# Three rounded products in place of float32 for most attention scores, and a later conversion of three weight blocks, in a one-core attention and feed-forward kernel

## The chip, the cores and the metric

The kernel runs on one core of one Trainium2 chip. Its engines are TensorE (PE in the profile; PEld is its weight load), VectorE (DVE), ScalarE (ACT), GpSimd (POOL) and SyncE (SP), which here issues most of the DMA transfers. Each engine works through its own queue in order; semaphores tie the queues together. The metric is the time of one execution in microseconds (us), as the median of the runs; a profiled execution gives the trace.

## The reference

Causal attention over 2 batches, 12 heads, 448 positions and 64 columns a head, then two feed-forward layers over the 768 columns, the first with a low-rank mixing of the positions in front, the second behind a layer norm:

```python
scores = scale * np.matmul(q, k.transpose(0, 1, 3, 2))
scores = np.where(mask, -1000000000.0, scores)
scores = scores - np.max(scores, axis=-1, keepdims=True)
attn = np.exp(scores); attn = attn / (np.sum(attn, axis=-1, keepdims=True) + 1e-09)
x = np.matmul(attn, v)                                    # heads side by side: 768 columns
h = x.transpose(0, 2, 1) @ U @ V                          # U: 448 x 32, V: 32 x 448
u = x + h.transpose(0, 2, 1); x = u + np.maximum(u @ w1a, 0.0) @ w2a
xn = (x - mean(x)) / np.sqrt(var(x) + 1e-06) * g_ln;      x + np.maximum(xn @ w1b, 0.0) @ w2b
```

The inputs q and k are drawn with a standard deviation of about 0.5. The weights arrive as 64-bit floats (the kernel reads their bits and makes 32-bit words of them).

## The kernel before, in words

The attention stage is written out by hand; the two feed-forward layers behind it are ordered by a planner (class `Plan`), which the change does not touch. The first 108 us of the profile are the attention stage.

Two heads form a *pair*, 12 pairs in all. Positions are cut into four blocks of 112. The main loop is `for n in range(NPT)`, here called round 0 to round 11. In round n, PE transposes the exponentials of pair n (`a_transpose`, L441), turns the finished outputs of pair n-1 back to positions by rows (`a_tokens`, L483), multiplies q and k of pair n+2 (`a_scores`, L387), multiplies pair n's transposed weights with v (`a_values`, L471), and from round 3 on adds the mixing of the positions for pair n-3 (`a_mix2`, L571). In odd rounds `a_sum` (L535) makes the small matrix `ts` that this mixing uses; its last step is a subtraction on DVE (L542). DVE takes the row maxima of pair n+2 from PSUM (`a_max`, L405, eight instructions, with the `ts` subtraction after the fifth), then the reciprocals (L461), and copies part of the transposes to SBUF (`pt`, L445). ACT takes the exponentials of pair n+1 (L422), spread over the round: one ahead of each of its copies in `a_transpose`, three more, then what `ahead("high", n)` puts in, then the rest. The transposes of pair n+1 need all eight of them.

Scores are float32 products. The two heads of a pair lie in the two halves of the 128 rows, so that their products use different halves of PE. Each float32 product is recorded as two passes.

While attention runs, the first four weight blocks of the first layer are loaded and converted. A block takes four steps: a load of 768 KB (SP), the upper half of each word (`upper`, ACT, L258), joining it with the middle (`joined`, DVE, L266), and `split` into a rounded high part (ACT, L299) and the low part `w - high` (L296). The products of the feed-forward layers take a weight and an activation each as such a high and a low part in float32r, three products for one. `ahead` sets in which round these steps are issued: the site "high" lies behind the sixth exponential and in front of `a_max`, the site "values" at the start of `a_values`. Before the change, upper halves go out in rounds 1, 3, 5, 7, joining in 2, 4, 6, 8, splitting in 3, 5, 7, 9, and the low parts of these four blocks are made by POOL. Two raw tiles hold the loads, so a joining is followed by the load of a later block.

The first products with these weights start in round 11: `mm1(early[0], 0, ...)` with block 0, after the loop `early[1]` with block 1 and `early[2]` with block 2 (L603). Between them stand the last pair's tokens, its own mixing (`a_mix1`, L553) and the last `a_mix2`. PSUM has 8 banks, taken in turn; a bank can be written again when all that read it are done.

q and k of a pair come as one tile of 128 rows and 2 x 448 columns, in three buffers; `a_load(n + 3)` at the end of `a_scores(n)` refills the buffer just read.

Of the kernel before, what the change touches and what calls it, by code (L numbers as in the profile page):

```python
# [8 lines left out]
F32 = mybir.dt.float32  # L9
F32R = mybir.dt.float32r  # L10
# [12 lines left out]
R = 32  # L23
# [14 lines left out]
PLACE_U, PLACE_W = 96, 192  # L38
MASKED = -8.0e9
LATE = 4  # L40
SLOTS = (1, 5, 6, 2, 7, 3, 4)

OFF = [Q * i * (i + 1) // 2 for i in range(NQ + 1)]
# [153 lines left out]
def block_kernel(ctx: ExitStack, tc: tile.TileContext, qk, v, U, V4, w1a, w2a, w1b, w2b, g_ln, out):  # L197
# [25 lines left out]
    def bank(name, i=None):  # L223
        if i is None:
            turn[0] += 1
        return ps.tile([P, 512], F32, tag="bank", name=name)
# [24 lines left out]
    def load_part(t, src, queue, r0=0):  # L251
        rows, cols = src.shape
        queue.dma_start(out=t[r0:r0 + rows].bitcast(U16)[:, :4 * cols - 1], in_=src.bitcast(U16)[:, 1:])
# [72 lines left out]

    def ahead(site, n):

        if site == "values" and n in (2, 4, 6, 8):
            plan.emit(first_w1[n // 2 - 1][2])  # L330
            plan.emit(next(loads))
        if site == "high" and n in (1, 3, 5, 7, 9):
            j = (n - 3) // 2
            if j >= 0:
                plan.emit(first_parts[j][0])
                plan.emit(first_parts[j][1], nc.gpsimd)
            if n < 9:
                plan.emit(first_w1[j + 1][1])

    qk_p = attn.enter_context(tc.tile_pool(name="qk_p", bufs=2))  # L340
    s_p = attn.enter_context(tc.tile_pool(name="s_p", bufs=6))
# [1 line left out]
    x_p = attn.enter_context(tc.tile_pool(name="x_p", bufs=2))  # L343
    ot_p = attn.enter_context(tc.tile_pool(name="ot_p", bufs=5))
    row_p = attn.enter_context(tc.tile_pool(name="row_p", bufs=3))
    sel_p = attn.enter_context(tc.tile_pool(name="sel_p", bufs=1))

    sc_t, qk_t, v_t, s_t, den_t, pt_t, x_t, o_t, rd_t, nm_t = ({} for _ in range(10))
    pairs = [(b, p) for b in range(B) for p in range(NP)]
# [2 lines left out]
    def a_load(n):  # L352

        if n >= NPT:
            return
        r = qk_t[n] = qk_p.tile([P, 2, S], F32, tag="qk", name=f"qk{n}", bufs=3)
        src = qk[n].rearrange("p (a h s) -> p a h s", a=2, h=2)
        for part in (slice(0, 2 * Q), slice(2 * Q, S)) if n == 0 else (slice(0, S),):
            for h in range(2):
                rows = slice(h * D, (h + 1) * D)  # L360
                (nc.scalar if h and n == 0 else nc.sync).dma_start(out=r[rows, :, part], in_=src[rows, :, h, part])

    def a_load_v(n):
        if n >= NPT:
            return
        t = v_t[n] = qk_p.tile([Q, NQ, 2, D], F32, tag="v", name=f"v{n}", bufs=3)
        nc.sync.dma_start(out=t, in_=v[n].rearrange("p (j h d) -> p j h d", j=NQ, h=2))
# [6 lines left out]
    def a_scores(n):  # L374
        if n >= NPT:
            return
        t = qk_t.pop(n)
        sc_t[n] = [bank("sc") for _ in JOBS]
        at = {(h, i): (acc, o) for acc, job in zip(sc_t[n], JOBS if n else FIRST) for h, i, o in job}
        if n:  # L380
            turn_of = lambda h, i: (3, 2, 0, 1).index(i)
        else:
            turn_of = lambda h, i: (i, 0) if i > 1 else (-1 - h, -i)
        for (h, i), (acc, o) in sorted(at.items(), key=lambda t: turn_of(*t[0])):
            w = (i + 1) * Q
            r = slice(h * D, (h + 1) * D)
            nc.tensor.matmul(  # L387
                acc[:Q, o:o + w], t[r, 0, i * Q:(i + 1) * Q], t[r, 1, :w], start=True, stop=True,
            )
        a_load(n + 3)  # L390


    def turns_of(n):
# [20 lines left out]
    def a_exp(n):  # L414

        if n >= NPT:
            return
        den = den_t[n] = small.tile([Q, 2, NQ], F32, tag="den", name=f"den{n}")
        nm, sb = nm_t.pop(n), s_t[n]
        for _, h, i, _ in turns_of(n):  # L420
            s = sb[h][:, OFF[i]:OFF[i + 1]]
            nc.scalar.activation(  # L422
                s, s, AF.Exp, bias=nm[:, h, i:i + 1], scale=-1.0, accum_out=den[:, h, i:i + 1]
            )
            yield
# [52 lines left out]
    def a_tokens(n):  # L478

        ot, rd = o_t[n], rd_t.pop(n)  # L480
        acc = bank("xt")
        for i in range(NQ):
            nc.tensor.transpose(acc[:Q, i * P:(i + 1) * P], ot[:, i * Q:(i + 1) * Q], ident)  # L483
        b, p = pairs[n]
        if p % 2 == 0:
            x_t[b, p // 2] = x_p.tile([Q, NQ, 2 * P], F32, tag="x", name=f"x{n}")
        x = x_t[b, p // 2]
        c = (p % 2) * P
        nc.vector.tensor_tensor(
            x[:, :, c:c + P].rearrange("p i (h d) -> p h i d", h=2),  # L490
            acc[:Q].rearrange("p (i h d) -> p h i d", i=NQ, h=2),
            rd.unsqueeze(3).to_broadcast([Q, 2, NQ, D]), ALU.mult,
        )
        if p % 2 == 1:

            queue = nc.gpsimd if n == NPT - 1 else nc.sync
            for i in range(NQ):
                t0, t_end = b * S + i * Q, b * S + (i + 1) * Q
                x0 = t0
                while t0 < t_end:  # L500
                    t1 = min(t_end, (t0 // P + 1) * P)
                    tb, rows, cols = t0 // P, slice(t0 % P, t0 % P + t1 - t0), slice((p - 1) * P, (p + 1) * P)
                    dst = y_sum["rim"][rows, cols] if tb == 3 else y_sum[b][rows, tb % 4, cols]
                    queue.dma_start(out=dst, in_=x[t0 - x0:t1 - x0, i])
                    t0 = t1
# [102 lines left out]
    with tc.manual_schedule():  # L608
# [10 lines left out]
        nc.gpsimd.memset(mhalf, -0.5)  # L619
        for g in range(4):  # L620
            nc.gpsimd.memset(odd[g * R:(g + 1) * R], -(g % 2))
        sel = sel_p.tile([P, 4, 4, R], F32, tag="sel", name="sel")
        nc.gpsimd.tensor_copy(
            sel, ident.rearrange("p (g r) -> p g r", g=4).unsqueeze(2).to_broadcast([P, 4, 4, R])
        )
# [10 lines left out]

        for g in range(4):
            load_part(first[1], V4[g * R:(g + 1) * R, g * Q:(g + 1) * Q], nc.sync, g * R)
        a_load(2)
        for n in range(3):  # L640
            a_load_v(n)
        warm = bank("warm")
        for n in range(WARM):
# [7 lines left out]
        early, early_i, low = {}, {}, None  # L651
        for n in range(NPT):
            exps = a_exp(n + 1)
            if n == 0:
                for k, cols in ((0, NQ * R), (1, Q)):
                    upper(first[k], tops[k], P if k else Q, cols)
            a_transpose(n, exps, low)
            if n > 2:
                a_rows(n - 3)
            if n:  # L660
                a_tokens(n - 1)
            if n == NPT - 2:
                a_reciprocals(n)
                ahead("last", n)
            mix = a_sum(n - 3) if n > 2 and n % 2 else None
            a_scores(n + 2)
            if n:
                row_load(n - 1)
            if n == 0:
                u_n = joined(uv[0][:Q, :NQ * R], first[0], tops[0]).rearrange("p (i r) -> p i r", i=NQ)  # L670
                nc.gpsimd.tensor_copy(
                    u_r.rearrange("p (i g r) -> p i g r", i=NQ, g=4), u_n.unsqueeze(2).to_broadcast([Q, NQ, 4, R])
                )
                v_n = joined(uv[1][:, :Q], first[1], tops[1])
                for _ in range(RAWS):
                    plan.emit(next(loads))
            if n == NPT - 1:
                early_i[0] = turn[0] % 8
                early[0] = bank("h")
                mm1(early[0], 0, 0, S, range(KC // 2))  # L680
            if mix:
                next(mix)
            if n == NPT - 1:
                mix_next = a_mix1(NPT - 2)
                a_rows(n - 2)
            for _ in range(3):
                next(exps, None)
            ahead("high", n)
            a_max(n + 2, mix)
            for _ in exps:  # L690
                pass
            if n == NPT - 1:
                whole(mix_next)
                mm1(early[0], 0, 0, S, range(KC // 2, KC))
            a_values(n)
            if n == 0:

                v_r = bank("vr")
                for g in range(4):
                    nc.tensor.matmul(  # L700
                        v_r[:, g * Q:(g + 1) * Q], sel[:, g].rearrange("p a r -> p (a r)"), v_n,
                        start=g == 0, stop=g == 3, skip_group_check=True,
                    )
                nc.scalar.copy(vs, v_r[:, :S])
                nc.vector.scalar_tensor_tensor(vs, f32(vs), odd, v_r[:, :S], ALU.mult, ALU.add)
                nc.gpsimd.memset(f32(vz).bitcast(U32), 0)
                nc.gpsimd.tensor_copy(vz[:, 0, :64], f32(vs[:, 384:448]))
                nc.gpsimd.tensor_copy(vz[:, 1, 64:], f32(vs[:, 0:64]))
            a_load_v(n + 3)
            if n > 1 and n % 2 == 0:  # L710
                a_quarters(n - 2)
            if n > 2:
                low = a_mix2(n - 3)
        rest = [low, a_mix2(NPT - 3), a_mix2(NPT - 2)]
        early_i[1] = turn[0] % 8
        early[1] = bank("h")
        mm1(early[1], 1, 0, S, range(KC // 2))
# [781 lines left out]
```

## Time and profile before

| | us |
|---|---|
| three runs | 742.59, 742.03, 741.73; median 742.03 |
| profiled execution, its span | 741.79, 740.0 |
| PE busy | 735.4 (99%) |
| DVE, ACT, POOL busy | 593.3, 520.0, 202.4 |
| DMA | 133.69 MB, 181 GB/s over the span |

Busy times are sums over the whole span; which engine another one waits for is seen in the chain of waits and in the timelines of a stretch. A row of a timeline gives the start, the time it took and the engine, then line, operation and tiles; what stands in brackets at its end is how long the engine was idle just before and what ended that.

### The profile page before, as it was taken

The page shows a single profiled execution, that of the slowest core. Times are in us where ns is not written, and L with a number is a line of the kernel's source. Part 1 is how long each engine was busy: PE and PEld are TensorE (multiplying, and loading weights), DVE is VectorE, ACT ScalarE, POOL GpSimd, SP SyncE. Part 2 cuts the span into 40 slices and gives each one's busy share as a digit, 9 for nine tenths or more (in the row PEclk, how much of TensorE's full clock was granted, in tenths as well). Part 3 has the DMA queues.
Part 4 walks back from the last instruction along what each step waited for, and adds up shares of the span by engine and source line. Part 5 has one row for each costly group of instructions (what it writes and reads, how often), then busy time and mean ns, then how long its engine had stood idle before and what let it go on. Part 6 is the DMA issues. An engine that isn't in the chain of part 4 may idle for free.

```text
span 740.0 us, 11873 instructions
## 1 busy us (share of the span) xinstructions
PE 735.4 (99%) x4240; PEld 687.0 (93%) x4240; DVE 593.3 (80%) x955; ACT 520.0 (70%) x961; POOL 202.4 (27%) x250
## 2 busy tenths in 40 slices
PE   9999999999999999999999999999999999999998
PEld 7676789999999999999999999999999999999998
DVE  6788749868969879879977989879868778788796
ACT  7999827466867777678773557578678677677762
POOL 3155430310430521512401201402402403315210
PEclk9999999999999999999999999999999999999999
DMA  8776526755893994987987346974966957969947
GB/s 202 203 214 186 149 57 237 185 133 150 157 237 130 168 235 105 224 194 174 215 211 272 135 171 178 252 188 79 221 180 129 233 162 153 228 186 164 258 83 187
DMA packets 55324, 133.69 MB, mean 181 GB/s; under 512 B 6866, under 2 KB 40354, under 8 KB 55266
## 3 DMA queue, kind: packets, MB, share of 16 engines
q1 hardware_dynamic: 30194, 98.82, 41.2%
q0 software_dynamic: 24784, 33.90, 31.1%
q8 instruction: 33, 0.54, 0.3%
q10 hardware_dynamic: 288, 0.23, 0.1%
q14 instruction: 25, 0.20, 0.1%
HBM read 91.79 MB, written 41.13 MB: 180 GB/s over the span
## 4 chain that ended last, share of the span: by engine, by line
PE 97%; DVE 1%; DMA 1%; ACT 0%; issue 0%; DVEq 0%
PE bank L914 27%; PE h L1113 14%; PE bank L1113 13%; PE h L914 7%; PE bank L995 7%; PE bank L972 5%; PE h L995 5%; PE bank L1147 5%; PE pv L471 3%; PE sc L387 3%; PE tr L441 3%; PE h L603 1%; DMA raw<-in_w1a 1%; PE h L972 1%; DVE s L405 1%; PE xt L483 1%
## 5 line engine op out<-in xcount | busy, mean ns | idle before, releaser
L1030 POOL DMA_DIRECT2D out_y<-part x88 | 77.0, 1049 | 221.0 <-ACT part L1026 209.8
L258 ACT CAST top<-raw 128x768 f16<-128x768 bf16 (+1 forms) x98 | 103.9, 1064 | 26.1 <-DMA raw<-in_w1b 12.4
L1030 POOL DMA_DIRECT2D ysum<-part x72 | 63.6, 990 | 195.5 <-ACT part L1026 176.5
L914 PE MATMUL bank<-u,w 128*128 128x448 f32 x549 | 114.7, 362 | 0.0
L1113 PE MATMUL h<-w,h 128*128 128x384 f32 (+1 forms) x576 | 109.6, 334 | 0.0
L914 PEld LDWEIGHTS bank<-u,w 128*128 128x128 f32 x549 | 102.8, 188 | 6.6
L1113 PE MATMUL bank<-w,h 128*128 128x384 f32 (+1 forms) x552 | 105.1, 335 | 0.0
L1113 PEld LDWEIGHTS h<-w,h 128*128 128x128 f32 x576 | 100.9, 188 | 0.2
L296 DVE TENSOR_TENSOR w<-xb,w 128x768 fp32r<-128x768 f32 x84 | 80.0, 954 | 24.4 <-ACT w L299 23.3
L1113 PEld LDWEIGHTS bank<-w,h 128*128 128x128 f32 x552 | 96.8, 188 | 0.3
L914 PE MATMUL bank<-s,w 128*128 128x448 f32 x459 | 95.5, 362 | 0.0
L296 DVE TENSOR_TENSOR w<-xa,w 128x768 fp32r<-128x768 f32 x74 | 69.7, 955 | 28.5 <-ACT w L299 28.3
L914 PEld LDWEIGHTS bank<-s,w 128*128 128x128 f32 x459 | 86.0, 187 | 5.7
L299 ACT CAST w<-xb 128x768 fp32r<-128x768 f32 x84 | 69.7, 836 | 24.3 <-DVE xb L266 12.3
L299 ACT CAST w<-xa 128x768 fp32r<-128x768 f32 x78 | 64.0, 836 | 18.7 <-DVE xa L868 15.0
L995 PE MATMUL bank<-w,h 128*128 128x384 f32 x288 | 63.0, 335 | 0.0
L1026 ACT COPY part<-h 128x384 f32<-128x384 f32 x79 | 37.2, 482 | 29.6 <-PE h L1113 13.4
L266 DVE SCALAR_TENSOR_TENSOR xa<-raw,top 128x768 uint32<-128x768 uint32 x48 | 45.2, 949 | 14.3 <-ACT top L258 14.2
L1026 ACT COPY part<-bank 128x384 f32<-128x384 f32 x91 | 42.3, 482 | 15.9 <-PE bank L1113 9.1
L422 ACT ACTIVATE s<-s,nm 112x336 f32<-112x336 f32 (+2 forms) x96 | 50.4, 533 | 2.4 <-DVE nm L405 2.4
L995 PEld LDWEIGHTS bank<-w,h 128*128 128x128 f32 x288 | 51.1, 188 | 0.0
L995 PE MATMUL h<-w,h 128*128 128x384 f32 (+1 forms) x216 | 50.5, 336 | 0.0
(150 smaller groups left out, 1247.8 us busy)
## 6 DMA issues: line engine op xcount, KB each, us to landing
raw<-in_w1a SPq DMA_DIRECT2D x24, 767.8 KB, 4.4
raw<-in_w2a SPq DMA_DIRECT2D x24, 767.8 KB, 5.8
raw<-in_w1b SPq DMA_DIRECT2D x24, 767.8 KB, 4.8
raw<-in_w2b SPq DMA_DIRECT2D x24, 767.8 KB, 7.3
out_y<-part POOLq DMA_DIRECT2D x88, 192.0 KB, 6.7
ysum<-part POOLq DMA_DIRECT2D x72, 192.0 KB, 6.4
qk<-in_qk SPq DMA_DIRECT2D x22, 224.0 KB, 5.1
v<-in_v SPq DMA_DIRECT2D x12, 224.0 KB, 4.3
```

Source lines behind the costliest of these rows:

```text
L258: nc.scalar.copy(halves[:, :, 1], words[:, :, 2].bitcast(BF16))
L266: nc.vector.scalar_tensor_tensor(x.bitcast(U32), middle, 13, top, ALU.logical_shift_right, ALU.bitwise_or)
L296: engine.tensor_tensor(w.t()[:, 1], src(), f32(w.t()[:, 0]), ALU.subtract)
L299: plan.op("ACT", ns[0], lambda: nc.scalar.copy(w.t()[:, 0], src()), cells, [w["hi"]]),
L422: nc.scalar.activation(s, s, AF.Exp, bias=nm[:, h, i:i + 1], scale=-1.0, accum_out=den[:, h, i:i + 1])
L914: nc.tensor.matmul(b.t()[:, :S], w.t()[:, a, p, kk * P:(kk + 1) * P], operand(c, kk), start=first and kk == a == c == 0, stop=kk == 2 and ...
L972: nc.tensor.matmul(b.t()[:, :t1 - t0], w.t()[:, a, k, c0:c0 + P], u[:, c, kk, t0:t1], start=kk == a == c == 0, stop=kk == KC - 1 and a == 1,)
L995: nc.tensor.matmul(accs[k].t()[:, :n], hs[j].t()[:, a, tb * P:(tb + 1) * P], flat(ws[j], c, k, n), start=j == a == c == 0 and not mix, sto ...
L1026: plan.op("ACT", 484, lambda: nc.scalar.copy(part.t(), b.t()[:, :HC]), [b[0]], [part[0]])
L1030: "POOL", 950, lambda: nc.gpsimd.dma_start(out=dst, in_=part.t(), accum_op=ALU.add), [part[0]],
L1113: nc.tensor.matmul(b.t()[:, :n], f.t()[:, a, c0:c0 + P], flat(w, c, p, n), start=first and p == a == c == 0, stop=p == 1 and a == 1, skip_ ...
L1147: nc.tensor.matmul(b.t()[:, :HC], rim.t()[:, a, 2 * k + p], w.t()[:, c, p], start=k == p == a == c == 0, stop=k == p == a == 1, skip_group ...
```

## The change

From pair 3 on (`EXACT = 3`), q and k are split by POOL into a rounded high part and a low part (`a_halves`, issued three rounds ahead of the pair's transposes: round n makes pair n+3's), and the scores are three float32r products, high by high, high by low and low by high, added up in PSUM. Pairs 0 to 2 stay float32. There are two buffers for q and k as loaded, two for high parts, one for low parts. The loads are issued elsewhere: `a_load(n + 4)` at the start of round n.

Of the first four weight blocks the first is converted as before (upper half in round 1, joining in 2, splitting in 3); for the others the steps stand in rounds 9, 10 and 11, the last split behind the loop. All four low parts go from POOL to DVE. The helper tile `sel` moves into the pool of x.

```diff
+UPPERS, JOINED, SPLITS = (1, 9, 10, 11), (2, 9, 10, 11), (3, 10, 11, 12)
+EXACT = 3
...
-        if site == "values" and n in (2, 4, 6, 8):
-            plan.emit(first_w1[n // 2 - 1][2])
+        if site == "values" and n in JOINED:
+            plan.emit(first_w1[JOINED.index(n)][2])
             plan.emit(next(loads))
-        if site == "high" and n in (1, 3, 5, 7, 9):
-            j = (n - 3) // 2
-            if j >= 0:
-                plan.emit(first_parts[j][0])
-                plan.emit(first_parts[j][1], nc.gpsimd)
-            if n < 9:
-                plan.emit(first_w1[j + 1][1])
+        if site == "high" and n in UPPERS:
+            plan.emit(first_w1[UPPERS.index(n)][1])
+        if site == "high" and n in SPLITS:
+            j = SPLITS.index(n)
+            plan.emit(first_parts[j][0])
+            plan.emit(first_parts[j][1], nc.vector)
...
-        r = qk_t[n] = qk_p.tile([P, 2, S], F32, tag="qk", name=f"qk{n}", bufs=3)
+        r = qk_t[n] = qk_p.tile([P, 2, S], F32, tag="qk", name=f"qk{n}", bufs=2)
...
+        sc_t[n] = [bank("sc") for _ in JOBS]
+        if n >= EXACT:
+            hi, lo = hl_t.pop(n)
+            for i in (3, 2, 0, 1):
+                w = (i + 1) * Q
+                for x, y in ((hi, hi), (hi, lo), (lo, hi)):
+                    for h in range(2):
+                        acc, o = next((acc, o) for acc, job in zip(sc_t[n], JOBS) for jh, ji, o in job if (jh, ji) == (h, i))
+                        r = slice(h * D, (h + 1) * D)
+                        nc.tensor.matmul(
+                            acc[:Q, o:o + w], x[r, 0, i * Q:(i + 1) * Q], y[r, 1, :w],
+                            start=i > 0 and x is y, stop=x is lo, skip_group_check=True,
+                        )
+            return
         t = qk_t.pop(n)
-        sc_t[n] = [bank("sc") for _ in JOBS]
...
-        a_load(n + 3)
+    hl_t = {}
+    def a_halves(n):
...
+        t = qk_t.pop(n)
+        hi, lo = hl_t[n] = [
+            qk_p.tile([P, 2, S], F32R, tag=f"qk{k}", name=f"qk{k}_{n}", bufs=2 - k) for k in range(2)
+        ]
+        nc.gpsimd.tensor_copy(hi, t)
+        nc.gpsimd.tensor_tensor(lo, t, f32(hi), ALU.subtract)
...
+        a_load_v(0)
         a_load(2)
-        for n in range(3):
+        for n in (1, 2):
             a_load_v(n)
...
+            if n:
+                a_load(n + 4)
...
             a_scores(n + 2)
+            if n == 0:
+                a_load(3)
+                a_load(4)
...
+            a_halves(n + EXACT)
...
         rest = [low, a_mix2(NPT - 3), a_mix2(NPT - 2)]
+        ahead("high", NPT)
```

DVE's queue in round 3, before: the copies and the scaled output x of pair 2 (`x_631`), then the row maxima of pair 5 (`ISA ... <-sc,mask`, each followed by a read of its result, `nm`).

```order
L445 COPY pt_2_603<-tr 112x448
L445 COPY pt_4_618<-tr 112x448
L489 TENSOR_TENSOR x_631<-xt,s_1_442 112x2x4x64
L405 ISA s_0_664,nm_663<-sc,mask 112x448
L405 ISA nm_663 112x1
L405 ISA s_1_665,nm_663<-sc,mask 112x448
```

The same place after; `w_717` is the first weight block in two parts, `xa_597` the joined block.

```order
L470 COPY pt_2_644<-tr 112x448
L470 COPY pt_4_659<-tr 112x448
L514 TENSOR_TENSOR x_672<-xt,s_1_460 112x2x4x64
L298 TENSOR_TENSOR w_717<-xa_597,w_717 128x768
L430 ISA s_0_721,nm_720<-sc,mask 112x448
L430 ISA nm_720 112x1
L430 ISA s_1_722,nm_720<-sc,mask 112x448
```

The low part of block 0 has come in between x and the first maximum. In ACT's queue in round 10, before, the exponentials of pair 11 follow each other without a break:

```order
L422 ACTIVATE s_0_1356,den_1391<-s_0_1356,nm_1355 112x336
L422 ACTIVATE s_0_1356,den_1391<-s_0_1356,nm_1355 112x112
L422 ACTIVATE s_1_1357,den_1391<-s_1_1357,nm_1355 112x336
L422 ACTIVATE s_1_1357,den_1391<-s_1_1357,nm_1355 112x112
L422 ACTIVATE s_0_1356,den_1391<-s_0_1356,nm_1355 112x224
```

After, two conversions stand behind the fourth: the upper half of block 2 (`top_102<-raw_599`) and the high part of block 1 (`w_1608`).

```order
L447 ACTIVATE s_0_1513,den_1551<-s_0_1513,nm_1512 112x336
L447 ACTIVATE s_0_1513,den_1551<-s_0_1513,nm_1512 112x112
L260 CAST top_102<-raw_599 128x768
L301 CAST w_1608<-xa_597 128x768
L447 ACTIVATE s_1_1514,den_1551<-s_1_1514,nm_1512 112x336
L447 ACTIVATE s_1_1514,den_1551<-s_1_1514,nm_1512 112x112
L447 ACTIVATE s_0_1513,den_1551<-s_0_1513,nm_1512 112x224
```

On DVE at the end of the loop, after: the reciprocals of the last pair are followed by the joining and the low part of block 3, and only then come the additions of the mixing (`ot<-mix`); before, the additions came next to the reciprocals.

```order
L486 RECIPROCAL rd_1638<-rd_1638 112x8
L268 SCALAR_TENSOR_TENSOR xa_597<-raw_1528,top_103 128x2x384
L298 TENSOR_TENSOR w_1746<-xa_597,w_1746 128x768
L599 TENSOR_TENSOR ot_1406<-mix,ot_1406 128x448
L599 TENSOR_TENSOR ot_1539<-mix,ot_1539 128x448
L607 TENSOR_TENSOR u<-ot_1406,u 128x448
L607 TENSOR_TENSOR u<-ot_1539,u 128x448
L514 TENSOR_TENSOR x_1685<-xt,rd_1638 112x2x4x64
```

Two instructions have come in front of the additions.

## Rows read from the trace of the kernel before

**Rows 1.** The page: busy time and share, and the granted clock by slices.

```profile
PE 735.4 (99%) x4240; PEld 687.0 (93%) x4240; DVE 593.3 (80%) x955; ACT 520.0 (70%) x961; POOL 202.4 (27%) x250
...
PEclk9999999999999999999999999999999999999999
```

**Rows 2.** Chain of waits, rounds 3 and 4: start, us, engine, tile, line.

```profile
34.36 2.08 PE sc L387 x16
36.44 2.04 PE pv L471 x16
38.48 0.40 PE mix L571
38.88 1.92 PE tr L441 x20
```

**Rows 3.** Groups by form: count | busy, mean ns of one.

```profile
L387 PE MATMUL sc<-qk 64*112 64x448 f32 x48 | 12.6, 575 | 0.0
```

**Rows 4.** Chain of waits: stretches of float32r products of 448, 384, 192 columns.

```profile
91.40 1.81 PE h L603 x9
...
733.34 2.08 PE bank L1113 x12
735.42 1.33 PE bank L1126 x12
```

**Rows 5.** Timeline of POOL, rounds 2 to 4.

```profile
30.78 1.81 POOL L516 TENSOR_TENSOR ot<-ot,row 128x448 f32<-128x448 f32 x1
37.39 1.84 POOL L296 TENSOR_TENSOR w<-xa,w 128x768 fp32r<-128x768 f32 x1 [4.80 <-ACT w L299]
...
41.29 0.56 POOL L576 CAST u<-ot 128x448 fp32r<-128x448 f32 x1 [1.75 <-DVE ot L574]
...
43.03 1.14 POOL L516 TENSOR_TENSOR ot<-ot,row 128x448 f32<-128x448 f32 x1
```

**Rows 6.** Timeline of ACT, rounds 2 and 3.

```profile
30.91 0.53 ACT L476 COPY ot<-pv 128x448 f32<-128x448 f32 x1 [0.52 <-PE pv L471]
...
36.47 0.84 ACT L299 CAST w<-xa 128x768 fp32r<-128x768 f32 x1
37.20 1.08 ACT L258 CAST top<-raw 128x768 f16<-128x768 bf16 x1
```

**Rows 7.** Timeline of DVE, rounds 2 and 3.

```profile
30.68 0.91 DVE L266 SCALAR_TENSOR_TENSOR xa<-raw,top 128x768 uint32<-128x768 uint32 x1
...
35.44 0.62 DVE L405 CUSTOM_DVE_ANT_0 s<-sc,mask 112x448 f32<-112x448 f32 x1 [0.69 <-PE sc L387]
...
37.70 0.43 DVE L542 TENSOR_TENSOR ts<-t,ts 64x256 fp32r<-64x256 f32 x1
```

**Rows 8.** The page's groups of instructions: DVE's low parts.

```profile
L296 DVE TENSOR_TENSOR w<-xb,w 128x768 fp32r<-128x768 f32 x84 | 80.0, 954 | 24.4 <-ACT w L299 23.3
```

**Rows 9.** Timeline of ACT, round 10 and behind the loop.

```profile
86.04 0.56 ACT L422 ACTIVATE s<-s,nm 112x336 f32<-112x336 f32 x1
...
87.34 0.19 ACT L422 ACTIVATION_READ_ACCUMULATOR s<-s,nm 112x1 f32 x1
...
98.06 0.54 ACT L476 COPY ot<-pv 128x448 f32<-128x448 f32 x1 [3.65 <-PE pv L471]
```

**Rows 10.** Chain of waits: round 11's transposes, and the last token mixing.

```profile
88.61 1.92 PE tr L441 x20
...
102.83 0.89 PE t L553 x8
```

**Rows 11.** Timeline of DVE behind the loop.

```profile
98.47 1.16 DVE L574 TENSOR_TENSOR ot<-mix,ot 128x448 f32<-128x448 f32 x2 [3.50 <-PE mix L571]
...
101.05 0.69 DVE L489 TENSOR_TENSOR x<-xt,rd 112x512 f32<-112x512 f32 x1 [0.16 <-PE xt L483]
```

**Rows 12.** Chain of waits, rounds 0 to 2: the first weight load.

```profile
15.35 7.23 DMA raw<-in_w1a
```

**Rows 13.** Timeline of SP, start.

```profile
8.10 1.52 SPq L367 DMA_DIRECT2D v<-in_v  x3
```

More of the change, by code (lines that the diff above doesn't have):

```diff
@@ L345, in block_kernel @@
     row_p = attn.enter_context(tc.tile_pool(name="row_p", bufs=3))
-    sel_p = attn.enter_context(tc.tile_pool(name="sel_p", bufs=1))
     sc_t, qk_t, v_t, s_t, den_t, pt_t, x_t, o_t, rd_t, nm_t = ({} for _ in range(10))
@@ L389, in a_scores @@
             )
-        a_load(n + 3)
+    hl_t = {}
+    def a_halves(n):
+        if n >= NPT:
+            return
+        t = qk_t.pop(n)
[4 more added lines that the diff above has]
+        nc.gpsimd.tensor_tensor(lo, t, f32(hi), ALU.subtract)
     def turns_of(n):
@@ L485, in a_tokens @@
         if p % 2 == 0:
-            x_t[b, p // 2] = x_p.tile([Q, NQ, 2 * P], F32, tag="x", name=f"x{n}")
+            x_t[b, p // 2] = x_p.tile([P, NQ, 2 * P], F32, tag="x", name=f"x{n}")[:Q]
         x = x_t[b, p // 2]
@@ L621, in block_kernel @@
             nc.gpsimd.memset(odd[g * R:(g + 1) * R], -(g % 2))
-        sel = sel_p.tile([P, 4, 4, R], F32, tag="sel", name="sel")
+        sel = x_p.tile([P, NQ, 2 * P], F32, tag="x", name="sel")[:, :2].rearrange("p i (g a r) -> p (i g) a r", g=2, a=4)
         nc.gpsimd.tensor_copy(
```

## Prediction

> **What bounds the kernel now.** I read the page's shares and slices first: TensorE (PE) is busy 99% of the span, with the granted clock in the top tenth in every slice [rows 1]. So what counts is what lengthens or shortens PE's own queue, and which wait holds it. The chain of waits says the same of the attention stage: from round 3 to round 4 it stays on PE, scores, values, mix, transposes, with no other engine between [rows 2]. An engine beside PE matters only when PE comes to wait for it. (The chain's clock reads 0.07 later than the timelines'; I take that off where I mix them.) The sum is made against the profiled execution, 741.79 us with a span of 740.0; the median of the runs is 0.24 higher, which my terms do not resolve.
>
> **Scores (gain).** A pair's scores are now 16 float32 passes on PE, 2.08 us from their start to that of the values [rows 2]. The two heads lie side by side: 48 passes of 575 ns fill only 12.6 us [rows 3]. A float32 pass costs 0.84 ns a column: two passes over 1120 columns make 1.88, so 0.20 of the 2.08 is the first weight load and the drain. (0.84 is two cycles at 2.4 GHz, the upper of the clock's two levels.) After, each head pair needs three float32r products per block. What such a product takes from start to start is in three stretches of pure float32r: 9 of 448 columns in 1.81, 201 ns; 12 of 384 in 2.08, 173; 12 of 192 in 1.33, 111 [rows 4]. Per column 0.43, so 152 for 336 columns; 224 lies between 104 (that slope) and 121 (between the last two rows), I take 107; 112 columns are held by the weight load, 96 ns, as in the 20 transposes of 1.92 [rows 2]. Three times 201 + 152 + 107 + 96 is 1.67, with 0.20 it is 1.87: 0.21 less a pair. Nine pairs (3 to 11): **-1.9**. The bounds: if side-by-side products carry no fixed cost the streams take 1.59 and it is -2.6; if the heads did not run together it would be twice 1.67, +1.46 a pair, +13.1. No row shows float32r on half the rows; the heads' float32 passes are the nearest, so I take -1.9.
>
> **POOL (hidden).** Each of these rounds adds a cast and a subtraction over 896 columns. Rows give 0.56 for a cast of 448, and 1.14 and 1.84 for subtractions and products of 448 and 768 [rows 5]: 1.1 and 2.1. With its other cast and two products of 1.14, POOL has 6.2 of about 7.1 us a round ((88.61 - 38.88)/7 [rows 2, 10]). The subtraction starts when the former pair's scores end and is done some 3.5 us before the next scores. PE's round covers it; without that cover each microsecond late costs nine.
>
> **The first block's low part moves from POOL to VectorE (DVE) in round 3 (loss).** In DVE's queue it now stands in front of the row maxima of pair 5. Those started at 35.44 [rows 7]. The low part needs the high part from ScalarE (ACT), a cast that started at 36.47 for 0.84, that is, ended at 37.31; POOL began on it at 37.39 [rows 5, 6]. ACT cannot be earlier: its work in the round follows from a copy at 30.91 which waited for PE [rows 6]. So DVE stands still until 37.39, works 0.95 [rows 8], and the maxima start at 38.34, 2.90 late. Queued behind them are all eight maxima, the ts subtraction among them, which ended at 38.13 [rows 7], the reciprocals and round 4's copies. PE's mix needs that subtraction: it ran at 38.41 (timeline clock), only 0.28 later. After, PE is there at 38.20 and the subtraction ends at 41.03: PE idles 2.8.
>
> It gets worse if DVE must also wait for POOL. In round 3 POOL's subtraction for pair 6 starts when PE's scores of pair 5 end, about 36.25, and takes 2.1, to 38.35; DVE's request at 37.39 falls inside. The trace shows one such meeting, the other way round: POOL's product at 30.78 took 1.81 instead of 1.14 while DVE's two-input joining ran from 30.68 to 31.59 [rows 5, 7]. If DVE is blocked likewise, the maxima start at 39.30 and PE idles 3.8. I take **+3.8**, since the one meeting that a row shows was a block; 2.8 is the other end.
>
> The Trainium skill ("SBUF — State Buffer", SBUF: two separate sides) states that a VectorE instruction with two SBUF inputs and a GpSimd instruction that reads SBUF exclude each other, whichever starts first holding the port to its end. By this rule the block holds in both directions, the term is 3.8 and the sum 745.4; without it 744.0. The 1.81 agrees with it.
>
> **Round 10 (loss).** ACT now gets the upper-half conversion of block 2 and the high cast of block 1 between the fourth and the fifth exponential of pair 11; before, the fifth followed at once (86.04) [rows 9]. The cast of 0.84 lets the next start after 0.73 (36.47 to 37.20), so 0.11 overlaps; the conversion of 1.08 [rows 6] then takes 0.97, both 1.7. The seventh exponential, which PE's second transpose of round 11 needs, was through at 87.53 [rows 9]; PE needed it at 88.64, 0.1 into its transposes [rows 10]. ACT and PE both follow from round 9's values, so the slack of 1.1 is all there is: **+0.6**. DVE's low part of block 1 meets POOL's 1.14 subtraction there, in front of copies that PE's first early block waits for: 0 to 1.2, I take **+0.4**.
>
> **After the last round (loss).** Block 3's high cast on ACT stands behind the copy at 98.06 [rows 9]; DVE's low part waits for it, in front of the two additions at 98.47, two subtractions and the scaled copy to x at 101.05 [rows 11]. In a row: cast from 98.5 to 99.3, low part to 100.3, additions and subtractions at 0.55 each to 102.5, x to 103.3 instead of 101.74. PE needs x at 102.76 [rows 10]: **+0.6**. Blocks 1 and 2 are ready long before PE wants them, and in rounds 5 to 9 ACT is relieved, which gives nothing since PE did not wait there.
>
> **The start.** The load of qk 2 now goes out behind that of v 0, one of three in 1.52, so 0.5 later [rows 13]; the scores of pair 2 wait for it. Against that one qk load fewer stands before the first weight block, whose landing after 7.23 us holds the chain [rows 12]. Between -0.4 and +0.7: **+0.1**. Two qk buffers in place of three are refilled a round ahead; no cost.
>
> **Sum:** -1.9 + 3.8 + 0.6 + 0.4 + 0.6 + 0.1 = +3.6; 741.79 + 3.6 = 745.4.
>
> **Rivals.**
> - *DVE is not blocked by POOL.* For it: the block seen was of POOL, not of DVE. Round 3 costs 2.8, round 10 only 0.6: 741.79 - 1.9 + 2.8 + 0.6 + 0.6 + 0.1 = 744.0. Chance 0.17.
> - *Not slower: the stall of round 3 is covered.* One mechanism: ACT reaches block 0's high cast before DVE is through with round 3's copies, about 34.7, so the maxima are late by 0.2 only. It decides once the cast ends before 35.5. Then 741.79 - 2.6 + 0.2 + 0.6 + 0.6 + 0.1 = 740.7 with the larger gain, 741.4 with the smaller. Against it: ACT would have to win about 2 us, and it is anchored to PE [rows 6]. It also stands for a wait that I have put on PE and that is not there. Chance 0.18.
> - *The clock falls.* PE would lie idle for the 3.8 us. If the granted clock then drops to the lower of its two levels, 1.2 GHz, for the transposes behind the stall, their 1.92 [rows 2] take twice as long: 745.4 + 1.9 = 747.3. Against it: every slice is at the upper level [rows 1], and no stall of that length stands in the trace. Chance 0.08.
> - *The heads do not run together in float32r.* 741.79 + 13.1 + 5.5 = 760.4. Chance 0.04.
>
> The Trainium skill ("TensorE: Matmul & The Clock Gate", What's actually happening) says that TensorE drops to half its clock when it has been idle. By that rule the clock rival is the likelier one; no row of this trace shows a drop.
>
> **How the numbers follow.** Forecast 0.53, own range 743.5 to 747.2; rivals 0.17, 0.18, 0.08, 0.04. What a measurement of this kernel tells from no change is 0.2%, 1.5 us: from 740.5 to 743.5 it is the same. The forecast, the first, third and fourth rival are slower, except for the edge of the first where the smaller stall meets the larger gain (744.0 - 0.7): slower 0.78. The covered stall lies about that line's other side: same 0.15, faster 0.07. The range leaves out the fourth rival and the faster half of the second: 741.8 to 748.0.
>
> **What would show it.** Right: scores of pairs 3 to 11 at about 1.87; in round 3 a low part on DVE in front of the maxima, idle before it until ACT's cast, and PE idle in front of pair 0's mix by about 3.8 (2.8: no block; 0: the step is wrong); a gap of 0.6 in round 11's transposes released by ACT; PE waiting for x before its last token mixing. Wrong: scores above 2.08, POOL as releaser of scores, a granted clock under 1.00 after round 3, or a round 4 that starts without a gap.

## The result, and the profile after

The changed kernel takes 749.52 us (749.18 to 749.63, four runs); the kernel before took 742.13 beside it (741.73 to 742.59, four runs). The ratio is 1.0099, with an interval from 1.0081 to 1.0116: slower by 7.4 us, where the prediction had 3.6 and a range that ends at 748.0. The profiled span is 747.8 us against 740.0.

The page of the changed kernel, the rows that answer to [rows 1]: shares, and the granted clock in 40 slices of 18.7 us.

```profile
PE 737.8 (99%) x4312; PEld 694.3 (93%) x4312; DVE 602.0 (81%) x959; ACT 520.0 (70%) x961; POOL 224.3 (30%) x264
...
PEclk9989999999999999999999999999999999999999
```

PE is busy 99% of the span as before, so the shares say nothing of 7 us. One digit does: the third slice, 37 to 56 us, has an 8 where before all were 9. PE's timeline shows where that is (start, duration, line, operation, forms; in brackets PE's idle time just before and what ended it).

```profile
34.23 0.46 PE L386 MATMUL sc<-qk 64*112 64x448 f32 x2
...
36.08 2.11 PE L496 MATMUL pv<-pt,v 112*64 112x448 f32 x16
41.98 0.71 PE L596 MATMUL mix<-vs,ts 128*128 128x448 f32 x1 [3.80 <-DVE ts L567]
42.49 3.94 PE L466 MATMUL tr<-ident,s 112*112 112x112 f32 x20
46.22 1.06 PE L508 MATMUL xt<-ident,ot 128*112 128x128 f32 x4
47.21 0.71 PE L386 MATMUL sc<-qk 64*112 64x448 f32 x2
```

From the values of round 3 (36.08) to pair 0's mix (41.98) pass 5.90 us, where it was 2.04 [rows 2]. After the gap the same 20 transposes run 3.73 us to the next row's start instead of 1.92, and the four of xt 0.99. The windows of 2 us show why (busy time and count by engine, then the granted clock):

```profile
38.00:40.00 2.00, 0.19 (x4) 0.00 (x0) 2.00 (x4) 0.84 (x4) 1.26 (x2) 1.00 0.81 299
40.00:42.00 2.00, 0.02 (x1) 0.05 (x1) 1.94 (x10) 0.64 (x2) 0.00 (x0) 0.85 1.05 282
42.00:44.00 2.00, 2.00 (x10) 1.86 (x11) 0.89 (x7) 0.52 (x2) 0.00 (x0) 0.50 0.58 117
...
46.00:48.00 2.00, 2.00 (x11) 1.59 (x11) 1.43 (x3) 2.00 (x10) 1.72 (x3) 0.50 0.74 165
48.00:50.00 2.00, 2.00 (x26) 1.54 (x26) 1.46 (x6) 0.54 (x3) 1.98 (x2) 0.95 1.02 277
```

PE did nothing from 38.2 on; before 42 the granted clock fell from 1.00 to 0.50, that is, from 2.4 to 1.2 GHz, and stayed there until about 48. The mean granted clock is 0.995 in each of the four runs, and 1.00 in the profile of the kernel before.

What held the mix, first in the chain of waits, then on POOL's timeline:

```profile
36.53 0.73 ACT w L301
...
37.28 1.96 DVE w L298
39.24 0.53 DVE s L430
...
41.41 0.44 DVE ts L567
...
41.98 0.71 PE mix L596
```
```profile
36.33 2.10 POOL L415 TENSOR_TENSOR qk<-qk,qk 128x896 fp32r<-128x896 f32 x1 [0.83 <-PE sc L386]
```

VectorE's low part waits for ScalarE's cast, starts at 37.28 and lasts 1.96 us where the page has 954 ns [rows 8]; POOL's subtraction is under way until 38.43. Behind it stand the maxima and the ts subtraction, 41.41 instead of 37.70 [rows 7].

The starts of the same groups on PE, before and after, up to the end of the attention stage, add up to 7.5 of the 7.8 us between the two profiled spans (the other 0.3 lies behind it):

| Stretch | forecast | measured |
|---|---|---|
| start, up to round 3 | +0.1 | +0.1 |
| scores of pairs 3 to 11 | -1.9 | -1.9 |
| gap in front of pair 0's mix | +3.8 | +3.9 |
| lower clock behind it | a rival | +2.9 |
| rounds 10 and 11 | +1.0 | +1.0 |
| behind the loop | +0.6 | +1.4 |
| sum | +3.6 | +7.5 |

The 2.9 is what mix, transposes, xt and scores took there (0.51, 3.73, 0.99, 2.31) less what they take at the upper clock (0.30, 1.92, 0.53, 1.85).

In round 10 ScalarE's two conversions (1.06 and 0.84) stand where the forecast had them, in front of the fifth exponential, and PE's transposes wait (ACT, then PE):

```profile
90.70 0.38 ACT L447 ACTIVATE s<-s,nm 112x112 f32<-112x112 f32 x1
...
91.08 1.06 ACT L260 CAST top<-raw 128x768 f16<-128x768 bf16 x1
91.98 0.84 ACT L301 CAST w<-xa 128x768 fp32r<-128x768 f32 x1
92.71 0.59 ACT L447 ACTIVATE s<-s,nm 112x336 f32<-112x336 f32 x1
...
94.28 2.04 PE L466 MATMUL tr<-ident,s 112*112 112x112 f32 x19 [0.36 <-ACT s L447]
```

Behind the loop, the timelines of POOL, VectorE and PE, the rows that answer to [rows 10, 11]:

```profile
100.25 2.28 POOL L541 TENSOR_TENSOR ot<-ot,row 128x448 f32<-128x448 f32 x2
...
100.67 2.69 DVE L298 TENSOR_TENSOR w<-xa,w 128x768 fp32r<-128x768 f32 x1 [1.86 <-ACT w L301]
...
105.97 0.96 DVE L298 TENSOR_TENSOR w<-xa,w 128x768 fp32r<-128x768 f32 x1 [0.90 <-ACT w L301]
106.96 1.16 DVE L599 TENSOR_TENSOR ot<-mix,ot 128x448 f32<-128x448 f32 x2
...
109.30 0.68 DVE L514 TENSOR_TENSOR x<-xt,rd 112x512 f32<-112x512 f32 x1
...
110.03 1.16 PE L578 MATMUL t<-x,u_r 112*128 112x128 f32 x8 [1.19 <-DVE x L514]
```

Block 2's low part lasts 2.69 beside two of POOL's products; the joining of block 3, its cast and its low part (105.97) are late by it, and x comes 1.19 too late for PE.

### The profile page after: what moved, and what is told of

It is laid out like the page before. It is cut to its first block, busy times and chain, and to the rows that moved or that the text cites. A ratio compares the mean times of both kernels' runs of the same rounds, so it can differ in the third digit from the quotient of the medians.

```text
span 747.8 us, 12044 instructions
## 1 busy us (share of the span) xinstructions
PE 737.8 (99%) x4312; PEld 694.3 (93%) x4312; DVE 602.0 (81%) x959; ACT 520.0 (70%) x961; POOL 224.3 (30%) x264
## 4 chain that ended last, share of the span: by engine, by line
PE 95%; DVE 3%; ACT 1%; issue 1%; DVEq 0%
PE bank L947 27%; PE h L1146 13%; PE bank L1146 13%; PE h L947 7%; PE bank L1028 7%; PE bank L1005 5%; PE h L1028 5%; PE bank L1180 5%; PE tr L466 3%; PE pv L496 2%; PE sc L386 2%; PE sc L400 1%; PE h L1005 1%; DVE w L298 1%; DVE s L430 1%
## 5 line engine op out<-in xcount | busy, mean ns | idle before, releaser
L298 DVE TENSOR_TENSOR w<-xa,w 128x768 fp32r<-128x768 f32 x78 | 77.2, 1003 | 35.9 <-ACT w L301 35.6
```

The source lines that it names most:

```text
L298: engine.tensor_tensor(w.t()[:, 1], src(), f32(w.t()[:, 0]), ALU.subtract)
```

## The experiments

Theory 1: the loss is VectorE held in round 3, the lower clock behind that gap, and late conversions in rounds 10 to 12. The rivals: the clock falls for another reason, or the time is lost in the new scores and on POOL. Times are medians; the kernel before took, beside them on the same chip, 741.95 for experiments 1, 2, 4 and 6, 742.09 for 3, 5, 7 and 8, and 742.03 for 9 and 10.

**1. Block 0's low part behind the maxima.**

```diff
             plan.emit(first_parts[j][0])
-            plan.emit(first_parts[j][1], nc.vector)
+            if j:
+                plan.emit(first_parts[j][1], nc.vector)
+        if site == "values" and n == SPLITS[0]:
+            plan.emit(first_parts[0][1], nc.vector)
```

> Block 0's low part stays on VectorE, but stands behind the maxima and reciprocals of round 3. Theory 1 (VectorE held in front of the maxima makes PE idle 3.9 us, and the lower clock behind that gap costs 2.5 more): both go, 749.5 - 3.9 - 2.5 = 743.1, granted clock at the upper level in every slice. Theory 2 (the clock falls for another cause, such as the new scores): only the gap goes, 745.6, with a drop still in round 3 or 4. Theory 3 (the time is lost elsewhere, the gap being covered by slack later): within 1 us of 749.5.

742.40 us, ratio 1.0006 (0.9997 to 1.0015): the two costs of round 3 are gone, and with them nearly the whole loss. PE's rows of round 3 and 4 now follow each other without a gap, and the transposes (37.99) are followed by xt at 39.91, after 1.92:

```profile
35.64 2.11 PE L499 MATMUL pv<-pt,v 112*64 112x448 f32 x16
37.68 0.48 PE L599 MATMUL mix<-vs,ts 128*128 128x448 f32 x1
37.99 2.08 PE L469 MATMUL tr<-ident,s 112*112 112x112 f32 x20
```

It is 0.7 better than expected, for two reasons: the lower clock had cost 2.9, not the 2.5 of the expectation, and the end costs 0.9 here, not 1.4, since block 2's low part lasts 1.58, not 2.69. Against that, the scores of round 5 take 2.44 instead of 1.85: PE waits 0.32 for POOL's subtraction, and POOL had waited 2.24 for pair 7's q and k.

**2. PE kept busy in the gap: four matmuls.**

```diff
         acc = bank("mix")
+        if n == 0:
+            for _ in range(FILL):
+                nc.tensor.matmul(acc[:, :S], still[:Q, :P], mask, start=True, stop=True)
```

> Four float32 matmuls of 448 columns whose result is not used stand in PE's queue in front of pair 0's mix, into the same bank: some 3.0 of the 3.9 us of the gap are filled. Nothing else moves. Theory 1 (the clock fell because PE was idle): VectorE's stall and the mix's start stay as they are, 41.98, but the transposes of round 4 take 1.9 and not 3.73: 749.5 - 2.5 = 747.0. Theory 2 (the clock fell for another cause): 749.5, transposes of round 4 still 3.7.

747.53 (747.23 to 749.24, five runs). In the profile the transposes of round 4 take 1.92 and the granted clock is 1.00 in every window of 2 us, so theory 1 holds. (The profile is of a run of 748.61, which also waits 1.16 for exponentials in round 1; the run of 749.24 has a mean granted clock of 0.998, the other four 0.999 or 1.00.) The edit was not as clean as intended: the added matmuls waited 1.66 for their bank and then put the mix off by 0.6.

**3. One matmul in the gap.** The same edit with one matmul instead of four.

> The changed kernel (749.5) with a single float32 matmul of 448 columns, 0.7 us, whose result is not used, in front of pair 0's mix; it can start when the first maxima free its bank, 1.7 us into the gap, and ends 1.4 before the mix. Nothing is delayed. If the clock fell because PE lay idle for 3.8 us at a stretch: 749.5 - 2.5 = 747.0, the transposes of round 4 at 1.9. If the sum of the idling counts, not the stretch: 749.5, transposes 3.7.

746.87 (746.34 to 750.04, six runs, two of them at 749.4 and 750.0, like the changed kernel). PE's rows in the profile:

```profile
40.08 1.02 PE L596 MATMUL mix<-mask,still 112*128 112x448 f32 x2 [1.65 <-DVE nm L431]
42.22 0.44 PE L600 MATMUL mix<-vs,ts 128*128 128x448 f32 x1 [1.12 <-DVE ts L568]
42.50 2.08 PE L467 MATMUL tr<-ident,s 112*112 112x112 f32 x20
```

From the values of round 3 the mix is 3.86 later than before, as in the changed kernel, so VectorE's wait is untouched; and yet 1.0 us of useless work in the middle saves 2.6: here the clock stays. So the clock is a cost of its own, and idling is its cause. The two long runs have a mean granted clock of 0.995, as the changed kernel has, and the other four 0.999: they lost the clock all the same. Why they did, no profile of theirs tells; one matmul does not hold the clock every time.

**4. The new scores alone.** The conversions' places of the kernel before, low parts on POOL again:

```diff
-        if site == "values" and n in JOINED:
-            plan.emit(first_w1[JOINED.index(n)][2])
+        if site == "values" and n in (2, 4, 6, 8):
+            plan.emit(first_w1[n // 2 - 1][2])
             plan.emit(next(loads))
...
+                plan.emit(first_parts[j][1], nc.gpsimd)
```

> The new scores with the conversion timetable of the kernel before (upper halves in rounds 1 to 7, low parts on POOL in rounds 3, 5, 7, 9). Theory 1 (the loss is all in the conversions' new places; POOL's added work is hidden): 742.1 - 9 x 0.23 = 740.0. Theory 2 (POOL cannot carry both: 6 us of halves and products a round, and 1.84 more in every second round of 7): the scores of rounds 4, 6, 8 wait for POOL by up to 0.9 each, 742 to 743, with POOL as releaser of scores.

747.56 (746.08 to 749.46): my expectation fell. The chain of waits in round 7, SyncE's queue (issues of pair 9's load behind a weight block), and PE's timeline:

```profile
56.12 8.22 DMA qk<-in_qk
...
64.47 0.94 POOL qk L414
...
65.48 2.10 POOL qk L415
...
67.62 2.79 PE sc L386 x22
```
```profile
54.39 0.54 SPq L254 DMA_DIRECT2D raw<-in_w1a  x1
...
55.49 1.23 SPq L361 DMA_DIRECT2D qk<-in_qk  x2
```
```profile
65.46 0.46 PE L386 MATMUL sc<-qk 64*112 64x448 f32 x2 [0.91 <-POOL qk L414]
67.62 0.83 PE L386 MATMUL sc<-qk,qk 64*112 64x448 f32 x4 [1.71 <-POOL qk L415]
```

The q and k that round 7 needs are pair 9's (the expectation of experiment 5 calls them pair 8's). They go out 1.1 us behind 768 KB of weights and take 8.2 us; POOL's halves, and PE's scores, wait for them. And the lower clock comes here too: PE idles 0.91 and 1.71, and from 68 to 70 the granted clock is 0.50. Together this costs 4.3 in round 7: from `t` (63.95) to the mix (72.87) pass 8.92 us, 4.65 in the kernel before. PE also waits in round 1 (1.02, for exponentials), in round 9 (0.47, for POOL) and at the end (0.69, for x). The change moves those weight loads to rounds 9 to 11 together with the conversions, so the two parts of the change need each other.

**5. The same, with the weight loads behind the q and k loads.**

```diff
         if site == "values" and n in (2, 4, 6, 8):
             plan.emit(first_w1[n // 2 - 1][2])
-            plan.emit(next(loads))
+        if site == "high" and n in (3, 5, 7, 9):
+            plan.emit(next(loads))
```

> As the run with the new scores alone (747.6), but each weight load after the first two goes out half a round later, behind the next pair's q and k in SyncE's queue, not in front. Theory 1 (that run lost because a q and k load of pair 8 stood behind a weight block, so POOL and then the scores of pair 8 came 3.8 us late): that wait goes, 747.6 - 3.8 = 743.8 or less. Theory 2 (POOL itself has too much work in those rounds): the scores still wait for POOL, within 1 us of 747.6.

744.04 (743.62 to 746.61): 3.5 less in the medians, 4.3 between the two profiled runs, and round 7 takes 4.65 from `t` to the mix. Pair 9's load now goes out in front of the weight block, so its place was the cause. (Pairs 8 and 10 stand 1.1 us behind a block here; their loads take 7.6 and 6.3 us but hold no scores for long.) The kernel is still 2 us over the kernel before. POOL has hardly a pause from 69.9 to 86, and PE waits for its subtraction: the scores of rounds 8 and 9 take 2.33 and 3.05 instead of 1.85:

```profile
69.89 2.11 POOL L416 TENSOR_TENSOR qk<-qk,qk 128x896 fp32r<-128x896 f32 x1
71.96 1.85 POOL L297 TENSOR_TENSOR w<-xa,w 128x768 fp32r<-128x768 f32 x1
...
78.76 2.09 POOL L416 TENSOR_TENSOR qk<-qk,qk 128x896 fp32r<-128x896 f32 x1
...
80.90 0.66 PE L387 MATMUL sc<-qk,qk 64*112 64x448 f32 x4 [0.94 <-POOL qk L416]
```

These two rounds use up 1.7 of the 1.9 us that the scores gain. Another 0.9 is lost before round 3's scores, 0.5 of it as a longer wait for exponentials in round 1, and about 1.0 is spread over rounds 4 to 7. Theory 2 of these two runs is true in part: with low parts and halves together POOL makes PE wait.

**6. The new places of the conversions alone**, with the float32 scores. The edit: the changed kernel's conversion sites put into the kernel before.

> The conversions' new places with the float32 scores of the kernel before, without POOL's halves. Theory 1: the low part of block 0 in front of the maxima still waits for ScalarE, without POOL's block a gap of 2.9 us; rounds 10 and the end cost 1.0 and 1.35 as in the changed kernel: 742.1 + 2.9 + 1.0 + 1.35 = 747.3 if 2.9 us of idling leave the clock, 749.8 if it falls as there. Theory 2 (the new scores bring the loss): within 1.5 us of 742.1.

748.63 (746.2 to 748.9, five runs; mean granted clock 0.999 in the run of 746.2, 0.997 or 0.998 in the others). The same kernel was run once more for a second profile.

> The run with the conversions alone once more, for a second profile: its five times were 746.2 and four from 748.2 to 748.9, and the profile was of the 746.2. If the 2.5 us between them are more time at the lower clock behind the gap of round 3 (there the mix to the scores of pair 6 lost 1.5), a profile of some 748.6 has the same gap of 2.6 and a lower clock for up to 2.5 us of work more. If they are another wait, the transposes of round 4 take 3.33 again, and PE waits elsewhere.

It took 747.71, and the kernel before 741.80 beside it. VectorE's and PE's timelines in the first profile, then PE's in the second:

```profile
36.96 0.96 DVE L297 TENSOR_TENSOR w<-xa,w 128x768 fp32r<-128x768 f32 x1 [2.60 <-ACT w L300]
...
40.66 0.44 PE L571 MATMUL mix<-vs,ts 128*128 128x448 f32 x1 [2.56 <-DVE ts L542]
40.94 3.33 PE L441 MATMUL tr<-ident,s 112*112 112x112 f32 x20
```
```profile
24.90 2.03 PE L441 MATMUL tr<-ident,s 112*112 112x112 f32 x19 [1.12 <-ACT s L422]
...
41.79 0.44 PE L571 MATMUL mix<-vs,ts 128*128 128x448 f32 x1 [2.56 <-DVE ts L542]
42.06 2.08 PE L441 MATMUL tr<-ident,s 112*112 112x112 f32 x20
```

Three things follow. The conversions make the loss without the new scores. Without POOL's halves the low part takes 0.96, and the mix comes 2.6 late and not 3.9: the 1.96 of the changed kernel is POOL's block. And behind the same gap of 2.56 the clock fell in one execution (3.33) and not in the other (2.08 in the row, 1.92 to the next start). The second expectation was wrong on one point: the first profile was of the 748.2 run, not of the 746.2. The second profile is 1.67 shorter from the mix to the next values, and 1.12 longer in round 1, where PE waits for exponentials; a run with neither comes to 747.7 - 1.1 = 746.6, close to the 746.2.

**7. Block 3's low part behind x.** On top of experiment 1:

```diff
-            if j:
+            if j in (1, 2):
                 plan.emit(first_parts[j][1], nc.vector)
...
         rest[2]()()
+        plan.emit(first_parts[3][1], nc.vector)
```

> As the run with block 0's low part behind the maxima (742.4), and block 3's low part on VectorE moved from in front of the last additions to behind them, behind x and the last half of pair 10's split. Theory 1 (PE's last wait, 0.59 in front of the token mixing of pair 11, is for x, and x is late because of that low part): the wait goes, 742.4 - 0.6 = 741.8. Theory 2 (x is late for another cause, POOL's row products or a late row load): 742.4, x still waited for.

741.37, ratio 0.9994 (0.9985 to 1.0002): PE's wait for x is gone, theory 1 of this run holds.

**8. No conversions in front of work that PE waits for.** On top of that:

```diff
-UPPERS, JOINED, SPLITS = (1, 9, 10, 11), (2, 9, 10, 11), (3, 10, 11, 12)
+UPPERS, JOINED, SPLITS = (1, 8, 9, 11), (2, 8, 10, 11), (3, 9, 11, 12)
+LOWS, LOADS = (3, 9, 11), (2, 9, 10, 11)
...
+        if site == "values" and n in LOWS:
+            plan.emit(first_parts[LOWS.index(n)][1], nc.vector)
```

> As the run before, and no conversion left in round 10 in front of exponentials: the upper half of block 1 in round 8, that of block 2 with block 1's high part in round 9, low parts behind the reciprocals of rounds 3, 9 and 11; weight loads where the changed kernel has them. Theory 1 (each of the small losses of rounds 10 to 12 is a conversion in front of work that PE waits for): the 0.2 and 0.6 of round 10 and the 0.75 of the end go, 742.4 - 1.5 = 740.9, which beats the kernel before. Theory 2 (VectorE and ScalarE have no room left in rounds 8 and 9): new waits there, 742.4 or more.

740.41, ratio 0.9979 (0.9970 to 0.9987): faster than the kernel before. PE has no wait left in rounds 10 to 12:

```profile
86.73 2.08 PE L468 MATMUL tr<-ident,s 112*112 112x112 f32 x20
...
100.95 1.05 PE L580 MATMUL t<-x,u_r 112*128 112x128 f32 x8
```

**9. These places with the float32 scores of the kernel before.** The edit: the conversion sites of experiment 8 put into the kernel before.

> The conversions placed as in the run that spread them (740.4), but with the float32 scores, three q and k buffers and idle POOL of the kernel before. Theory 1 (the new scores are worth 0.22 for each of nine pairs, and conversions so placed cost nothing): 740.4 + 2.0 = 742.4, the kernel before within 0.5. Theory 2 (the 1.7 won there came from the conversions' places or from elsewhere): 740.5 to 741.

742.27, ratio 1.0000 (0.9990 to 1.0009): conversions so placed cost nothing, and the gain of experiment 8 is the new scores'.

**10. Pair 2's q and k in front of pair 0's v.** On top of experiment 8:

```diff
-        a_load_v(0)
         a_load(2)
-        for n in (1, 2):
+        for n in range(3):
             a_load_v(n)
```

> As the run that spread the conversions (740.4), but the load of pair 2's q and k in front of that of pair 0's v, as in the kernel before. Theory 1 (scores of pair 2 come 0.5 earlier, but PE then waits as much longer for the exponentials in round 1, so the start costs nothing either way): within 0.4 of 740.4. Theory 2 (the later load costs its 0.5 in full): 739.9.

740.06, ratio 0.9973 (0.9964 to 0.9982). The 0.35 to experiment 8 is less than either interval is wide: inconclusive between the two theories, and the shortest median of all.

## Why the prediction was wrong

**The failed step is the clock.** The prediction forecast the gap (3.8, measured 3.86, by way of the mechanism it named) and then priced the work behind it at the upper clock; the fall stood beside it as a rival of 0.08 at +1.9. It belonged into the sum: the forecast gap and the rival were one event, in all four runs of the changed kernel (mean clock 0.995). A granted clock under 1.00 after round 3, one of the prediction's own signs of being wrong, is what the profile shows. "No stall of that length stands in the trace" was used as evidence against, but a trace without such a stall says nothing of what follows one. Experiments 2 and 3 show the cause, experiment 1 the price. The price was also too small, since it counted the transposes alone: mix, xt and scores ran at the lower clock too, 2.9 in all. The Trainium skill ("TensorE: Matmul & The Clock Gate", What's actually happening) says that an idle TensorE goes to half its clock, and the trace agrees: 0.50 from 42 to 48 us. This should have weighed more than the absence of such a row.

**The scores: right.** 1.85 us a pair from pair 5 on, forecast 1.87; -1.9 over nine pairs (pair 6 counted at the upper clock), and 740.41 against 742.27 between experiments 8 and 9. Pairs 3 and 4 took 1.98 and 2.12, only 0.10 and 0.07 less than before; why is open. That the sum still fits is in part luck: pair 6 gained 0.34, since it had taken 2.19 and not 2.08. The bound of 1.59 for the streams does not follow from its rows (the slope of 0.43 alone makes 1.44 of three times 1120 columns); the term taken does not rest on it.

**POOL: right for this kernel.** Nowhere in its profile does PE wait for POOL (in experiment 1, with the gap gone, it does once, 0.32). Cast and subtraction take 0.93 and 2.10, forecast 1.1 and 2.1. Experiment 5 shows the edge: with one low part of 1.85 more in every second round PE waits for POOL in rounds 8 and 9.

**Round 3's gap: right, with POOL's block.** The low part took 1.96, and 0.96 without POOL's halves (experiment 6). The Trainium skill ("SBUF — State Buffer", SBUF: two separate sides) has the lock in both directions, and so has the trace: VectorE is the one held here, POOL was in [rows 5].

**Rounds 10 and 11: right in sum.** 0.58 for the exponentials (forecast 0.6), 0.17 in round 10's values and 0.26 in the early blocks (forecast 0.4). Experiment 8 removes all of it.

**Behind the loop: mis-sized.** Forecast 0.6, measured 1.4. The working had block 3's cast directly behind the ot copy. It came later, because VectorE joined block 3 only after block 2's low part, which POOL's two products held for 2.69. The block was thought of in two places and forgotten in the third. Experiment 7 shows the wait for x to be block 3's low part.

**The start: right in sum, in part by luck.** +0.1. The later load cost what the working says: the scores of pair 2 take 2.61 to the next row instead of 2.08. Most of it came back in round 1, where PE's wait for exponentials is gone. But that rests on one execution: this wait was 0.33 in the profile of the kernel before and 1.12 in one run of experiment 6, which has the same loads at the start as that kernel.

## What to carry to other kernels

A stall of a few us on a TensorE that is otherwise full is not priced by its length alone: price the work behind it at half the clock too, unless something keeps the engine busy. Here 3.8 us of idling brought the lower clock in all four runs of the changed kernel, and 2.6 us in one of the two profiles of experiment 6. When work moves to an in-order queue, what matters is what stands behind it: the same low part cost 6.8 us in front of the maxima (3.9 of gap, 2.9 of clock) and no wait of PE behind the reciprocals. Before calling two parts of a change separable, look at what each frees for the other, SyncE's queue included.

## What the runs showed that was not expected

The same gap of 2.56 us, in two executions of one kernel, brought the lower clock in one and left it at 1.00 in the other. After gaps of 1.65 and 1.12 with one matmul between, it stayed in the profiled run of experiment 3 and, by their mean clock, in three others, but not in the other two; after 0.91 and 1.71 with two matmuls between, it fell in experiment 4. So these runs give no length of a gap from which on the clock falls. With the waits of round 1, this accounts for the spread of the kernel of experiment 6, 746.2 to 748.9, as far as two profiles can.

A load of q and k (two halves of 224 KB) took 8.2 us when it was issued 1.1 us behind one of 768 KB in the same queue. In the same place it took 6.4 us for another pair of experiment 4 and 7.6 and 6.3 us in experiment 5, and 4.0 to 5.0 us in these two runs, from round 2 on, where no weight block stood just in front.
